# Three real products in place of four for batch 0's complex weight product, in a Fourier and maxout kernel

## The chip, the cores and the metric

The kernel runs on one core of one Trainium2 chip. The metric is the device time of one execution in microseconds (us); the time before is the median of three runs, and one further execution was profiled.

## What is computed

`x` holds 8 batches of 3072 rows by 256 columns. Each batch goes through a real Fourier transform along its rows, a complex 256 x 256 weight product with a bias, a soft threshold and the inverse transform; a maxout layer (three 256 x 768 products, their maximum, one 768 x 256 product) follows.

```
X = rfft(x, axis=1);  Xr, Xi = X.real, X.imag
Yr = Xr @ w_r - Xi @ w_i + b_r
Yi = Xr @ w_i + Xi @ w_r + b_i
Yr, Yi = sign(Y) * max(abs(Y) - 0.01, 0)      # each of the two
y = irfft(Yr + 1j * Yi, n=3072, axis=1)
h = max(y @ w1, y @ w2, y @ w3);  out = h @ w_out
```

## The kernel before

The transform of length 3072 is split as 96 x 32. For each batch the stages are: `pa`, a 96-point product along n1 (tile `a_d` in DRAM holds the result); `px`, a 32-point product along n2, in 12 groups of four frequencies; `py`, the complex weight product; the threshold; `pz`, the inverse over n2 (tile `z_d` in DRAM); `pi`, the inverse over n1; then `pu` and `pd`, the maxout layer. Batches 1 to 7 work with pairs of f16 tiles. Batch 0 goes ahead of everything in f32, because the scales that the f16 pairs need don't exist yet, and while it runs the weights are loaded (`rw`, `ru`) and put into shape by VectorE, GpSimd and ScalarE. Nothing of the maxout layer can begin before batch 0's inverse, so TensorE passes through the 12 groups of batch 0 first, and the 1630 us after them are the eight maxout layers with batches 1 to 7 woven in.

One step of batch 0's loop issues, for group k: `first_b(k+1)` (the `px` matmuls, and two ScalarE copies into `tf`, one of them negated), `first_w(k)` (eight `py` matmuls: for each of two halves j and each of two row blocks h one with `w_r` and one with `w_i`; VectorE then adds `bias` at L750, ScalarE makes the two halves of the threshold at L760 and L761, VectorE subtracts them at L762) and `first_q(k-1)` (one `pz` matmul over all 128 rows; ScalarE copies it to `zs` and sends it to `z_d`). The last group, k = 11, has its own matrices. Every engine works through its own list in order; the order within a list was fixed when the program was built, and a table (`planned(k, ...)`) says at which step the work on the maxout weights is handed in. That work has four phases for each pair of weight blocks: GpSimd scales a copy (L402, `lower`), VectorE joins the two words of a float64 (L408 and L411, `combine`; L416, `join`), and `finish` subtracts one weight from another on VectorE (L423) and splits the difference into f16 halves.

The PSUM tiles of this part are handed out in turn from three pools, `ff`, `up` and `dn`, with 3, 3 and 2 banks: a tile of `dn` takes the bank of the tile six places before it, one of the others that of the tile nine places before.

Of the kernel before, what the change touches and what calls it, by code (L numbers as in the profile page):

```python
# [25 lines left out]
def dft_tables():  # L26
# [51 lines left out]
    mq = [np.block([[u, z], [z, v]])[order] for u, v in ((q, q), (q, qs))]  # L78
    even, odd = (np.pad(fa[0:48, np.arange(96) % 4 // 2 == i], ((0, 16), (0, 16))) for i in (1, 0))
# [22 lines left out]
def fourier_maxout_kernel(  # L102
# [5 lines left out]
    P = 128  # L108
# [94 lines left out]
    qf = const.tile([P, 2, P], F32, name="qf")  # L203
# [47 lines left out]

    def load_tables():
        rows = [b.rearrange("(r o d) -> r o d", r=1, o=1) for b in (b_r, b_i)]
# [5 lines left out]
        nc.sync.dma_start(out=st["tiled"], in_=mq[:, 26])  # L259

    def load_last_bias():
        rows = [b.rearrange("(r o d) -> r o d", r=1, o=1) for b in (b_r, b_i)]
        for c in range(2):
            nc.sync.dma_start(out=bias[64 * c:64 * c + 64, 1:2], in_=rows[c].broadcast_to([64, 1, D]))
        nc.gpsimd.dma_start(out=bias[96:97, 1:2], in_=rows[0])
# [59 lines left out]
    def scale_bias():  # L325
        mb = small("mxb")
        nc.vector.tensor_reduce(
            out=mb, in_=bias[:, 0], axis=AX.X, op=ALU.max, apply_absolute_value=True
# [25 lines left out]
    class Weights:  # L354
# [33 lines left out]
        def phases(self, n):  # L388
# [30 lines left out]

            def finish():  # L420
                if self.less:
                    other = self.raw[n + 2][:, :, :, 1].bitcast(F32)
                    nc.vector.tensor_tensor(out=m, in0=m, in1=other, op=ALU.subtract)  # L423
                split_scaled(hi, lo, m, self.sc)

            return (lower, combine, join, finish) if hi is not None else (lower, combine, join)
# [285 lines left out]
    def first_b(k):  # L712
        aj = st.pop(("a", k))
        px = ff_tile("px")
        pv = px.rearrange("p (h j m) -> p h j m", h=KD, j=2)
        for j in range(2):
            for h in range(KD):
                nc.tensor.matmul(
                    pv[:, h, j], aj[:, j, h * P:(h + 1) * P], mb_f[:, 2 * k + j], start=True, stop=True
                )  # L720
        st["t", k] = t = fft.tile([P, KD, 384], F32, name="tf", tag="t2", bufs=2)
        tv = t.rearrange("p h (j m) -> p (h j) m", j=2)
# [7 lines left out]
        if k == NJP - 1:  # L730
            st["ts"] = s_tile("tsf").rearrange("p (h m) -> p h m", h=KD)
            st["late"] = nc.gpsimd.tensor_copy(out=st["ts"], in_=t[:, :, 192:320])
            for z in (32, 96):
                nc.gpsimd.memset(st["ts"][:, :, z:z + 1], 0.0)

    def first_w(k):
        last = k == NJP - 1
        t = st.pop(("t", k)).rearrange("p h (j m) -> p h j m", j=2)
        py = ff_tile("py")
        pv = py.rearrange("p (j d) -> p j d", j=2)  # L740
        for j in range(2):
            for h in range(KD):
                t2 = st["ts"][:, h] if last and j == 1 else t[:, h, j, 0:P]
                r, i = (fft_weights[h][:, n * D:n * D + D] for n in range(2))
                nc.tensor.matmul(pv[:, j], t[:, h, j, 64:192], r, start=h == 0, stop=False)
                nc.tensor.matmul(pv[:, j], t2, i, start=False, stop=h == KD - 1)
        u = fft.tile([P, 2, D], F32, name="uf", tag="vh", bufs=3)
        bv = bias if last else bias[:, 0:1, :].broadcast_to([P, 2, D])
        mx = batch(0, "u")
# [18 lines left out]
    def first_q(k):  # L768
        u = st.pop(("v", k))
        pz = ff_tile("pz")  # L770
        pv = pz.rearrange("p (j d) -> p j d", j=2)
        if k < NJP - 1:
            nc.tensor.matmul(pz, qf[:, 0], u.rearrange("p j d -> p (j d)"), start=True, stop=True)
        else:
# [757 lines left out]
```

## Time and profile before

| | us |
|---|---|
| median of three runs | 1742.47 (1741.91 to 1744.53) |
| the profiled execution, its own time | 1737.65 |
| its span, first to last instruction | 1735.9 |
| TensorE busy | 1713.4 (99%) |
| VectorE busy | 1269.0 (73%) |
| ScalarE busy | 1169.1 (67%) |
| GpSimd busy | 292.2 (17%) |

Busy shares are means over the whole span; what one stage waits for is read from the rows further down. PE is TensorE, PEld its weight loads, DVE VectorE, ACT ScalarE, POOL GpSimd, SP SyncE (DMA issues only). An f32 matmul leaves two records, one for each of its two passes.

### The profile page before, as it was taken

The page shows a single profiled execution, that of the slowest core. Times are in us where ns is not written, and L with a number is a line of the kernel's source. Part 1 is how long each engine was busy: PE and PEld are TensorE (multiplying, and loading weights), DVE is VectorE, ACT ScalarE, POOL GpSimd, SP SyncE. Part 2 cuts the span into 40 slices and gives each one's busy share as a digit, 9 for nine tenths or more (in the row PEclk, how much of TensorE's full clock was granted, in tenths as well). Part 3 has the DMA queues.
Part 4 walks back from the last instruction along what each step waited for, and adds up shares of the span by engine and source line. Part 5 has one row for each costly group of instructions (what it writes and reads, how often), then busy time and mean ns, then how long its engine had stood idle before and what let it go on. Part 6 is the DMA issues. An engine that isn't in the chain of part 4 may idle for free.

```text
span 1735.9 us, 42087 instructions
## 1 busy us (share of the span) xinstructions
PE 1713.4 (99%) x16171; PEld 1278.0 (74%) x16171; DVE 1269.0 (73%) x2690; ACT 1169.1 (67%) x2493; POOL 292.2 (17%) x523
## 2 busy tenths in 40 slices
PE   8999999999999999999999999999999999999998
PEld 5866777677776777777777777777777777778998
DVE  2887887687866788678876688757787467667775
ACT  4567676677766777667775777667776566666775
POOL 2101012111221212211221111211222110110000
PEclk9999999999999999999999999999999999999999
DMA  9866565577646767466766567555753443422121
GB/s 294 249 183 195 161 167 162 159 183 190 186 120 178 181 185 192 133 175 177 191 168 167 156 178 204 159 143 153 191 160 106 121 126 104 122 78 64 56 60 34
DMA packets 203863, 269.61 MB, mean 155 GB/s; under 512 B 31438, under 2 KB 153262, under 8 KB 203566
## 3 DMA queue, kind: packets, MB, share of 16 engines
q1 hardware_dynamic: 171294, 193.34, 42.4%
q0 software_dynamic: 24736, 66.62, 12.0%
q10 hardware_dynamic: 7632, 6.95, 1.4%
q8 instruction: 128, 2.10, 0.5%
q14 instruction: 73, 0.60, 0.1%
HBM read 124.31 MB, written 75.50 MB: 115 GB/s over the span
## 4 chain that ended last, share of the span: by engine, by line
PE 81%; DVE 9%; DMA 5%; ACT 4%; issue 1%; SPq 1%; ACTq 0%; POOL 0%; DVEq 0%; POOLq 0%
PE pu L184 11%; PE pu L186 11%; PE pu L185 11%; PE pd L184 8%; PE pd L186 8%; PE pd L185 8%; PE py L184 3%; PE py L186 3%; PE py L185 3%; PE pi L1091 2%; PE px L792 2%; PE pa L625 2%; PE pz L960 2%; PE pu L1176 2%; PE pa L642 1%
## 5 line engine op out<-in xcount | busy, mean ns | idle before, releaser
L184 PE MATMUL pu<-yh,wuh 128*128 128x384 f16 x1344 | 438.6, 326 | 0.0
L186 PE MATMUL pu<-yh,wul 128*128 128x384 f16 x1344 | 438.0, 326 | 0.0
L185 PE MATMUL pu<-yl,wuh 128*128 128x384 f16 x1344 | 438.0, 326 | 0.0
L184 PE MATMUL pd<-woh,hh 128*128 128x256 f16 x1152 | 314.1, 273 | 0.6 <-ACT o L1273 0.4
L186 PE MATMUL pd<-woh,hh 128*128 128x256 f16 x1152 | 313.8, 273 | 0.1
L185 PE MATMUL pd<-wol,hh 128*128 128x256 f16 x1152 | 313.8, 273 | 0.0
L176 DVE TENSOR_TENSOR hh<-h,hh 128x384 f16<-128x384 f32 x336 | 185.9, 553 | 110.2 <-ACT hh L175 109.9
L1142 ACT ACTIVATE pu<-pu 128x384 f32<-128x384 f32 x336 | 160.7, 478 | 145.1 <-PE pu L186 135.1
L175 ACT ACTIVATE hh<-h 128x384 f16<-128x384 f32 x336 | 174.4, 519 | 70.2 <-DVE h L1146 64.9
L186 PEld LDWEIGHTS <-wul 128*128 128x128 f16 x1344 | 131.4, 98 | 86.7
L635 POOL DMA_DIRECT2D a_d<-aq x160 | 94.9, 597 | 584.9 <-ACT aq L632 573.5
L184 PEld LDWEIGHTS <-wuh 128*128 128x128 f16 x1344 | 131.3, 98 | 83.3 <-issue 21.6
L1278 POOL DMA_DIRECT2D out_dram<-o x189 | 104.5, 559 | 449.2 <-ACT o L1273 446.0
L185 PEld LDWEIGHTS <-wuh 128*128 128x128 f16 x1344 | 131.4, 98 | 62.5 <-issue 1.0
L1150 ACT ACTIVATE h<-pu 128x384 f32<-128x384 f32 x226 | 109.4, 484 | 47.1 <-PE pu L186 42.7
L184 PE MATMUL py<-wch,tt 128*128 128x256 f16 x504 | 137.4, 273 | 0.6 <-ACT aq L632 0.3
L186 PE MATMUL py<-wch,tt 128*128 128x256 f16 x504 | 137.3, 273 | 0.0
L185 PE MATMUL py<-wcl,tt 128*128 128x256 f16 x504 | 137.3, 272 | 0.0
L184 PEld LDWEIGHTS <-hh 128*128 128x128 f16 x1152 | 112.6, 98 | 33.0 <-issue 11.8
L185 PEld LDWEIGHTS <-hh 128*128 128x128 f16 x1152 | 112.7, 98 | 21.5 <-issue 0.5
L1105 DVE SCALAR_TENSOR_TENSOR y<-pi,ye 128x192 f32<-128x192 f32 x252 | 110.4, 507 | 21.8 <-ACT ye L1099 21.6
L186 PEld LDWEIGHTS <-hh 128*128 128x128 f16 x1152 | 112.6, 98 | 13.8 <-DVE hh L176 0.4
(288 smaller groups left out, 3551.0 us busy)
## 6 DMA issues: line engine op xcount, KB each, us to landing
zq<-z_d SPq DMA_DIRECT2D x63, 384.0 KB, 4.7
out_dram<-o POOLq DMA_DIRECT2D x189, 128.0 KB, 3.5
ab<-a_d SPq DMA_DIRECT2D x84, 256.0 KB, 4.3
ab<-ab SPq DMA_DIRECT2D x336, 64.0 KB, 2.8
vb<-vb SPq DMA_DIRECT2D x308, 64.0 KB, 2.9
z_d<-zs POOLq DMA_DIRECT2D x70, 256.0 KB, 3.9
xm<-in_x_dram SPq DMA_DIRECT2D x40, 384.0 KB, 4.3
a_d<-aq POOLq DMA_DIRECT2D x160, 96.0 KB, 3.3
```

Of the source, the lines that this page charges most:

```text
L175: nc.scalar.activation(out=hi, in_=src, func=AF.Copy)
L176: later(lambda: nc.vector.tensor_tensor(out=lo, in0=src, in1=h, op=ALU.subtract))
L184: nc.tensor.matmul(o, lh, rh, start=start, stop=False, **kw)
L185: nc.tensor.matmul(o, lh, rl, start=False, stop=False, **kw)
L186: st["mm"] = nc.tensor.matmul(o, ll, rh, start=False, stop=stop, **kw)
L625: st["mm"] = nc.tensor.matmul(pa[r][64 * h:64 * h + 64], ft[rows, t], xt[rows, i, h], start=t == i, stop=t == 1,)
L635: nc.gpsimd.dma_start(out=av[1 - r, :, :, n:n + 512], in_=o[64 * h:64 * h + 48])
L792: nc.tensor.matmul(pv[:, h, :, g // 2, g % 2], ah[:, g // 2, g % 2, h * P:(h + 1) * P], mb_sb[:, i, 4 * kb + g].rearrange("p (c m) -> p c ...
L1105: nc.vector.scalar_tensor_tensor(out=yv[:, e], in0=pv[:, 0], scalar=(1 - 2 * e) * Y_SCALE, in1=ev, op0=ALU.mult, op1=ALU.add,)
L1142: st["act"] = nc.scalar.activation(out=p, in_=p, func=AF.Relu)
L1150: st["act"] = nc.scalar.activation(out=h32, in_=p, func=AF.Relu, scale=H_SCALE)
L1278: nc.gpsimd.dma_start(out=out_v[b, c, t + i], in_=o[:, i])
```

## The change

For groups 0 to 10 of batch 0 the complex product is made from three real ones: (Xr + Xi) times `w_r`, Xi times -(`w_r` + `w_i`), and Xr times (`w_i` - `w_r`). `add_fft_weights` makes the two sums of weights on VectorE. GpSimd makes Xr + Xi (L745). The first product (`pc`) is copied out by ScalarE (`cs`, L772), GpSimd adds it to the bias (L774), and VectorE adds the two others (L800). The real and imaginary parts now lie side by side in the columns, so the inverse over n2 is four matmuls on 64 rows each, two into each of two PSUM tiles, and it runs two groups behind instead of one. The subtraction of maxout weights goes from VectorE to GpSimd (L436), and the table of planned work has new numbers. Group 11 keeps its form.

```
 def first_b(k):
...
+    if k < NJP - 1:
+        pv = px.rearrange("p (h c j m) -> p h j c m", h=KD, c=2, j=2)
...
+    if k < NJP - 1:
+        nc.scalar.activation(out=t[:, :, 0:256], in_=px.rearrange("p (h m) -> p h m", h=KD), func=AF.Copy)
+        nc.gpsimd.tensor_tensor(
+            out=t[:, :, 256:384], in0=t[:, :, 0:128], in1=t[:, :, 128:256], op=ALU.add
+        )
+        return
...
+def first_sum(k):
+    pc = ff_tile("pc")[:, 0:D]
+    first_product(pc, st["t", k], 2, [fft_weights[h][:, 0:D] for h in range(KD)])
+    c1 = s_tile("cs")
+    nc.scalar.activation(out=c1, in_=pc, func=AF.Copy)
+    st["u", k] = u = fft.tile([P, 2, D], F32, name="uf", tag="vh", bufs=3)
+    nc.gpsimd.tensor_tensor(
+        out=u, in0=bias_ri, in1=c1.rearrange("p (o d) -> p o d", o=1).broadcast_to([P, 2, D]), op=ALU.add
+    )
...
+        first_sum(k)
+        t, bv = st.pop(("t", k)), st.pop(("u", k))
+        pv = py.rearrange("p (c d) -> p c d", c=2)
+        first_product(pv[:, 0], t, 1, st["ws"][0])
+        first_product(pv[:, 1], t, 0, st["ws"][1])
...
 def first_q(k):
     u = st.pop(("v", k))
-    pz = ff_tile("pz")
-    pv = pz.rearrange("p (j d) -> p j d", j=2)
     if k < NJP - 1:
-        nc.tensor.matmul(pz, qf[:, 0], u.rearrange("p j d -> p (j d)"), start=True, stop=True)
...
+        pz = [ff_tile("pz")[:, 0:D] for _ in range(2)]
+        for c in range(2):
+            for j in range(2):
+                rows = slice(64 * j, 64 * j + 64)
+                nc.tensor.matmul(pz[j], qf[rows, 2 + c], u[rows, c], start=c == 0, stop=c == 1)
+        return pz
...
-        for c in range(2):
-            nc.sync.dma_start(out=bias[64 * c:64 * c + 64, 0:1], in_=rows[c].broadcast_to([64, 1, D]))
-        nc.sync.dma_start(out=qf, in_=mq[:, 0:2])
+        for c, v in enumerate((b_r, b_i)):
+            row = v.rearrange("(o d) -> o d", o=1)
+            nc.sync.dma_start(out=bias_ri[:, c], in_=row.broadcast_to([P, D]))
+        nc.sync.dma_start(out=qf, in_=mq[:, 0:4])
...
-    for n in range(0, 6, 2):
-        planned(n - 1, phase, w_up, n)
-        planned(n, prepare, w_up, n)
-        if n < 4:
-            planned(5 + n // 2, phase, w_up, n)
+    for k, n in ((1, 0), (2, 2), (5, 4)):
+        planned(k - 1, phase, w_up, n)
+        planned(k, prepare, w_up, n)
+    for k, n in ((4, 0), (6, 2)):
+        planned(k, phase, w_up, n)
+    for k, n in ((6, 0), (7, 2)):
+        planned(k, phase, w_up, n)
...
-        (load_a, k + 3), (load_a, k + 4), (stage_b, k + 1), (stage_w, k), (finish_w, k), (stage_q, k - 1),
+        (load_a, k + 3), (load_a, k + 4), (stage_b, k + 1), (stage_w, k), (finish_w, k), (stage_q, k - 2),
+        (stage_q, k - 1 if k == NJP else -1),
```

VectorE's list at the beginning of batch 0's loop, before: L750 adds the bias to `py` of a group, L373 finds the largest value of a loaded weight block `rw`, L762 ends the threshold (rows that only read an accumulator are left out here and below).

```order
L750 ISA uf_278,mxu_279<-py_269,bias_89 128x512
L373 TENSOR_REDUCE mwu_96<-rw_241 128x2
L762 ISA uf_278,mxu_279<-uf_278,t_281 128x512
L750 ISA uf_321,mxu_279<-py_312,bias_89 128x512
L373 TENSOR_REDUCE mwu_96<-rw_254 128x2
```

The same place after the change, from the first weight block to the end of group 0's threshold; L800 is now the addition of the bias, L812 the end of the threshold, and the names of `rw` are those of the first three blocks and then the fourth.

```order
L387 TENSOR_REDUCE mwu_96<-rw_245 128x2
L387 TENSOR_REDUCE mwu_96<-rw_258 128x2
L387 TENSOR_REDUCE mwu_96<-rw_300 128x2
L422 TENSOR_SCALAR xhl_303<-xhl_303 128x768
L422 TENSOR_SCALAR xhl_354<-xhl_354 128x768
L425 SCALAR_TENSOR_TENSOR rw_245<-rw_245,xhl_303 128x768
L425 SCALAR_TENSOR_TENSOR rw_258<-rw_258,xhl_354 128x768
L800 ISA uf_278,mxu_271<-py_272,uf_278 128x512
L430 SCALAR_TENSOR_TENSOR rw_245<-rw_245 128x768
L800 ISA uf_321,mxu_271<-py_315,uf_321 128x512
L387 TENSOR_REDUCE mwu_96<-rw_348 128x2
L812 ISA uf_278,mxu_271<-uf_278,t_285 128x512
```

Before, group 0's addition stood ahead of the first weight block; now three blocks' maxima and four passes over the first two stand ahead of it.

TensorE's list around group 0's inverse, before: `py_312` is group 1's product (its last two of eight matmuls), `pz_327` group 0's inverse, `pt_334` a small transpose for a scale, `px_357` group 3 and `py_365` group 2.

```order
L745 MATMUL py_312<-wst_132,tf_266 128x256
L746 MATMUL py_312<-wst_132,tf_266 128x256
L773 MATMUL pz_327<-uf_278,qf_73 128x512
L278 MATMUL pt_334<-id_sb_76,col_288 128x128
L718 MATMUL px_357<-mb_all_77,aj_244 128x128 x4
L745 MATMUL py_365<-wst_132,tf_309 128x256
```

The same place after the change: `py` and `pc` of groups 0, 1 and 2 are 272 and 273, 315 and 316, 366 and 367, `px` of groups 3 and 4 is 358 and 403, and pz_383 and pz_384 are group 0's inverse.

```order
L764 MATMUL py_315<-wch_79,tf_268 128x256 x4
L292 MATMUL pt_332<-id_sb_76,col_292 128x128
L764 MATMUL pc_273<-wst_132,tf_255 128x256 x2
L764 MATMUL pc_316<-wst_132,tf_268 128x256 x2
L764 MATMUL py_366<-wch_79,tf_312 128x256
L764 MATMUL pc_367<-wst_132,tf_312 128x256
L738 MATMUL px_358<-mb_all_77,aj_248 128x2x64 x4
L764 MATMUL pc_367<-wst_132,tf_312 128x256
L764 MATMUL py_366<-wch_79,tf_312 128x256 x3
L738 MATMUL px_403<-mb_all_77,aj_261 128x2x64
L825 MATMUL pz_383<-uf_278,qf_73 128x256
L825 MATMUL pz_384<-uf_278,qf_73 128x256
```

Group 0's inverse stood right behind group 1's `py`; it has moved behind `pc`, `px` of group 3 and the whole of group 2's product.

GpSimd's list after the change, from its first addition on: L745 makes a group's sum in `tf` (255, 268 and 312 are groups 0 to 2), L416 is the scaling of a weight block that was L402, L774 adds the bias.

```order
L745 TENSOR_TENSOR tf_255<-tf_255 128x2x128
L745 TENSOR_TENSOR tf_268<-tf_268 128x2x128
L416 TENSOR_SCALAR xhl_303<-rw_245 128x768
L416 TENSOR_SCALAR xhl_354<-rw_258 128x768
L774 TENSOR_TENSOR uf_278<-bias_ri_90,cs_276 128x512
L416 TENSOR_SCALAR xhl_500<-rw_300 128x768
L745 TENSOR_TENSOR tf_312<-tf_312 128x2x128
L774 TENSOR_TENSOR uf_321<-bias_ri_90,cs_319 128x512
```

Before, the list held only the L416 rows (as L402) here; group 2's sum now stands behind the scaling of the third weight block.

## Rows read from the trace of the kernel before

**Rows 1.** Busy us (instructions) by stretch: PE, PEld, DVE, ACT, POOL, clock, DMA, GB/s.
```profile
30.00:40.00 10.00, 10.00 (x56) 8.69 (x55) 4.31 (x12) 4.85 (x12) 0.91 (x1) 1.00 1.04 369
50.00:60.00 10.00, 10.00 (x49) 8.01 (x49) 10.00 (x20) 5.54 (x10) 2.27 (x3) 1.00 1.01 347
```

**Rows 2.** TensorE's waits from 29 to 104 us: total, times, longest, in us.
```profile
PE pz L773 <- DVE mxu L762: 1.0, 1, 1.0
PE pi L1041 <- ACT zh L1028: 0.5, 1, 0.5
```

**Rows 3.** TensorE's timeline: start, us, instruction; batch 0's loop and its end.
```profile
29.14 2.02 PE L718 MATMUL px<-mb_all,aj 128*128 128x128 f32 x16 [3.25 <-DMA aj<-a_d]
31.00 0.66 PE L745 MATMUL py<-wst,tf 128*128 128x256 f32 x2
...
78.43 1.05 PE L718 MATMUL px<-mb_all,aj 128*128 128x128 f32 x8
79.32 0.60 PE L745 MATMUL py<-wst,tf 128*128 128x256 f32 x2
...
82.78 1.02 PE L773 MATMUL pz<-uf,qf 128*128 128x512 f32 x2
83.63 0.38 PE L278 MATMUL pt<-id_sb,col 128*128 128x128 f32 x2
...
103.81 0.91 PE L1041 MATMUL pi<-xm,zh 96*128 96x96 f16 x11 [0.53 <-ACT zh L1028]
```

**Rows 4.** TensorE's timeline around matmuls on 48 of 128 rows, four places of the array.
```profile
336.89 0.27 PE L186 MATMUL pd<-woh,hh 128*128 128x256 f16 x1
337.09 0.84 PE L625 MATMUL pa<-xhl,zeros 48*64 48x512 f16 x12
337.86 0.34 PE L184 MATMUL pu<-yh,wuh 128*128 128x384 f16 x1
```

**Rows 5.** DMA issues from 33.2 to 33.6 us: size, us to landing.
```profile
rw<-in_moe_w_dram SPq DMA_DIRECT2D x1, 768.0 KB, 9.5
```

**Rows 6.** VectorE's timeline from 42 to 50 us, and one row later on.
```profile
42.83 0.94 DVE L373 TENSOR_REDUCE mwu<-rw 128x2 f32<-128x768 f32 x1
43.69 1.02 DVE L408 TENSOR_SCALAR xhl<-xhl 128x768 uint32<-128x768 uint32 x2
44.62 0.95 DVE L411 SCALAR_TENSOR_TENSOR rw<-rw,xhl 128x768 uint32<-128x768 uint32 x1
45.49 0.68 DVE L750 CUSTOM_DVE_ANT_1 uf<-py,bias 128x512 f32<-128x512 f32 x1
...
49.03 0.68 DVE L762 CUSTOM_DVE_ANT_0 uf<-uf,t 128x512 f32<-128x512 f32 x1
49.64 0.95 DVE L416 SCALAR_TENSOR_TENSOR rw<-rw 128x768 uint32<-128x768 uint32 x1
...
64.02 1.39 DVE L762 CUSTOM_DVE_ANT_0 uf<-uf,t 128x512 f32<-128x512 f32 x1
```

**Rows 7.** GpSimd's timeline: two of its instructions.
```profile
36.41 0.91 POOL L402 TENSOR_SCALAR xhl<-rw 128x768 f32<-128x768 f32 x1 [11.31 <-DMA rw<-in_moe_w_dram]
...
63.73 1.14 POOL L402 TENSOR_SCALAR xhl<-rw 128x768 f32<-128x768 f32 x1 [1.88 <-DVE ru L411]
```

**Rows 8.** ScalarE's groups, 20 to 104 us: busy us, mean ns, idle before.
```profile
L945 ACT ACTIVATE zs<-pz 128x512 f32<-128x512 f32 x12 | 7.1, 590 | 13.5 <-PE pz L773 13.0 <-issue 0.4
L726 ACT ACTIVATE tf<-px 128x256 f32<-128x256 f32 x12 | 4.5, 377 | 0.0
```

**Rows 9.** TensorE's timeline in its first 26 us, and stretches at the span's end.
```profile
1.32 4.02 PE L1297 MATMUL idle<-zeros 128*128 128x512 f16 x9 [1.32 <-POOL zeros L1292]
20.11 5.78 PE L1297 MATMUL idle<-zeros 128*128 128x512 f16 x26
...
1731.00:1733.00 2.00, 0.21 (x2) 0.00 (x0) 0.48 (x1) 0.84 (x2) 0.00 (x0) 1.00 0.02 6
1733.00:1735.90 2.90, 0.00 (x0) 0.00 (x0) 0.00 (x0) 0.00 (x0) 0.00 (x0) 0.75 0.39 132
```

More of the change, by code (lines that the diff above doesn't have):

```diff
@@ L263, in load_last_bias @@
         for c in range(2):
-            nc.sync.dma_start(out=bias[64 * c:64 * c + 64, 1:2], in_=rows[c].broadcast_to([64, 1, D]))
+            for j in range(2):
+                nc.sync.dma_start(
+                    out=bias[64 * c:64 * c + 64, j:j + 1], in_=rows[c].broadcast_to([64, 1, D])
+                )
         nc.gpsimd.dma_start(out=bias[96:97, 1:2], in_=rows[0])
@@ L327, in scale_bias @@
         nc.vector.tensor_reduce(
-            out=mb, in_=bias[:, 0], axis=AX.X, op=ALU.max, apply_absolute_value=True
+            out=mb, in_=bias_ri.rearrange("p c d -> p (c d)"), axis=AX.X, op=ALU.max, apply_absolute_value=True
         )
@@ L729, in first_b @@
         )
[L730 to L734, printed above, removed]
+        st["ts"] = s_tile("tsf").rearrange("p (h m) -> p h m", h=KD)
+        nc.gpsimd.tensor_copy(out=st["ts"], in_=t[:, :, 192:320])
+        for z in (32, 96):
+            nc.gpsimd.memset(st["ts"][:, :, z:z + 1], 0.0)
@@ new lines, in first_product @@
+    def first_product(o, t, part, w):
+        for h in range(KD):
+            nc.tensor.matmul(
+                o, t[:, h, part * P:(part + 1) * P], w[h], start=h == 0, stop=h == KD - 1
+            )
+    def first_sum(k):
[6 more added lines that the diff above has]
+            out=u, in0=bias_ri, in1=c1.rearrange("p (o d) -> p o d", o=1).broadcast_to([P, 2, D]), op=ALU.add
+        )
@@ L736, in first_w @@
     def first_w(k):
         last = k == NJP - 1
-        t = st.pop(("t", k)).rearrange("p h (j m) -> p h j m", j=2)
+        mx = batch(0, "u")
         py = ff_tile("py")
[L740 to L746, printed above, removed]
@@ L747, in first_w @@
-        u = fft.tile([P, 2, D], F32, name="uf", tag="vh", bufs=3)
-        bv = bias if last else bias[:, 0:1, :].broadcast_to([P, 2, D])
-        mx = batch(0, "u")
+        if last:
+            t = st.pop(("t", k)).rearrange("p h (j m) -> p h j m", j=2)
+            pv = py.rearrange("p (j d) -> p j d", j=2)
+            for j in range(2):
+                for h in range(KD):
+                    t2 = st["ts"][:, h] if j == 1 else t[:, h, j, 0:P]
+                    r, i = (fft_weights[h][:, n * D:n * D + D] for n in range(2))
+                    nc.tensor.matmul(pv[:, j], t[:, h, j, 64:192], r, start=h == 0, stop=False)
+                    nc.tensor.matmul(pv[:, j], t2, i, start=False, stop=h == KD - 1)
+            u = fft.tile([P, 2, D], F32, name="uf", tag="vh", bufs=3)
+            bv = bias
+        else:
+            first_sum(k)
[3 more added lines that the diff above has]
+            first_product(pv[:, 1], t, 0, st["ws"][1])
+            u = bv
@@ L1384, in fourier_maxout_kernel @@
                 pump()
-    with tc.issue_after(st["late"].ins):
-        for c, v in enumerate((b_r, b_i)):
-            row = v.rearrange("(o d) -> o d", o=1)
-            nc.gpsimd.dma_start(out=bias_ri[:, c], in_=row.broadcast_to([P, D]))
     quiet = st["power"].ins, st["zs"].ins
```

59 lines of the change are left out of this document (38 added, 21 removed).

## The prediction

> **What bounds the kernel now.** I read the busy time by stretch first [rows 1]. While batch 0's groups run, TensorE is busy in all of each 10 us at clock 1.00; VectorE fills its stretch as well from 50 to 60 us, and the DMA engines are at a share of 1.0 at 347 to 369 GB/s. The waits [rows 2] say who decides: between 29 and 104 us TensorE waits 1.0 us once for VectorE's L762 and 0.5 us once for the first `pi`, besides the wait for its first data. So batch 0's part lasts as long as TensorE's own matmuls, from 29.14 us to the first `pi` at 103.81 [rows 3]. Behind that TensorE is busy 99% of the span, so a shift of the first `pi` should reach the end nearly whole. In a group [rows 3] four `px` take 0.89 us (78.43 to 79.32), eight `py` 3.46 (79.32 to 82.78), thus 0.433 for one of 256 columns, and `pz` with 512 columns 0.85 (82.78 to 83.63). The reader is to see that this is a TensorE bound with VectorE close behind, so a saving on TensorE counts only while no other engine is late.
>
> **1. Six products for eight.** Two fewer in each of 11 groups: 22 x 0.433 = **-9.5 us**.
>
> **2. The inverse.** One matmul of 512 columns (0.85) becomes four of 256 columns on 64 rows. Each has two passes of 0.216 (half of 0.433). No row of before shows f32 on 64 rows. The nearest [rows 4] are twelve f16 matmuls of 512 columns, each at one of four places of the array: they take 0.77 us (337.09 to 337.86), where one after the other would take 12 x 0.22 = 2.7 (26 such on the full array take 5.78 [rows 9]); so matmuls at different places do overlap, three rounds of 0.22 being 0.67, and 0.1 is lost, with another 0.1 ahead (336.89 to 337.09 for a spacing of 0.11). Bounds for the four: 0.86, if the two halves of the array work side by side throughout (no cost), and 1.73 + 0.2 = 1.93, if they don't at all: 11 x 1.08 = +11.9. I take the middle way. TensorE starts matmuls in order, and both passes of one use the same rows, so the next one, on the other rows, can start only with the second pass; four then need five pass times, 1.08, plus 0.2 for the change to and fro: 1.28, 11 x 0.43 = **+4.7 us**. On this the Trainium skill (TensorE: Matmul & The Clock Gate, Part 3) says that matmuls on distinct row groups run concurrently, some 4 ns apart. No run here shows that for f32; by it the four would cost 0.86 + 0.2, the term would be +2.3, and the sum 2.4 us lower.
>
> **3. The start of the loop.** Here I put most of the time, because the list of VectorE has changed. Its first L800 (group 0's bias, once L750 behind group 0's `py`) now stands behind the maximum of the third weight block, two L422 and two L425. The third block was issued at 33.2 to 33.6 and took 9.5 us to land [rows 5]; VectorE read it at 42.83 [rows 6]. Ahead of it SyncE now asks for 256 KB more (both biases on 128 rows instead of 64, 128 KB, and twice the `qf`, 128 KB): at 369 GB/s [rows 1] 0.7 us, so 43.5. Then, by the starts in [rows 6], 0.86 for the maximum, 0.93 for two L422 (as L408), 2 x 0.87 for two L425 (as L411), 0.61 for L800: group 0's addition ends at **47.6**. Before, the addition of group 2 already began at 45.49.
>
> TensorE gets there earlier. From 31.00 [rows 3]: `py` of group 0 1.73, `px` 0.89, `py` of group 1 1.73, `pt` 0.2, four `pc` 1.73, and one `py` of group 2, whose `tf` ScalarE writes behind `pc` of group 0: about 38.0. The next `pc` needs group 2's sum, which GpSimd makes behind the scaling of the third block (43.5 + 0.9 [rows 7] + some 0.6). Then `px` of group 3 needs a PSUM bank: counted through the program (`px` and `py` of group 0 are the 19th and 21st tile, and so on), it is the 27th, in `dn`, and takes the bank of the 21st, `py` of group 0, which L800 sets free at 47.6. So TensorE stands from 38.0 to 47.6 but for one `pc`: **+9.2 us** (8.5 if the extra bytes delay nothing, 10.2 if GpSimd slows VectorE by 1 us here). Behind it `pz` of group 0 needs L812: 47.6 + 0.87 (L430, as L411) + 0.61 + 0.86 + 0.68 = 50.6, about when TensorE comes to it.
>
> **4. The old waits go.** With TensorE late, L762's 1.0 us goes; all ten `pa` matmuls (0.85 each) now stand behind the last `pz`, where eight left 0.5 us uncovered: **-1.5 us** (to 0).
>
> **5. Waits later on.** Followed further by the same durations, both lists stay close: `pc` of group 4 takes the bank of `py` of group 3, and comes 0.9 us before its L800. The other banks and the `pz` have 2 to 5 us in hand. **+1.0 us** (0 to 4, rival C).
>
> **6. The clock.** The trace's one low clock is at its end [rows 9]: after the last matmul, 0.2 us into 1731 to 1733, the stretch 1733.00 to 1735.90 has 0.75, a mean of 1.00 and the lower of the two levels, 1.2 GHz. The idle time at 26 us, 3.25 us long [rows 3], kept 1.00. The new one has 7 us without a matmul, so I expect the clock at 1.2 GHz when work resumes. What that costs is seen at the program's start [rows 9]: nine matmuls of 512 columns in 4.02 us, 0.45 each instead of 0.22. Some 4 us at half speed lose **+2.0 us** (0, if it stays up, to 2.8, if all of the 2.8 us ahead of group 0's `pz` takes twice as long).
>
> **What costs nothing.** The four weight sums on VectorE fall ahead of the loop; even from 30 to 40 us it is busy only 4.31 us [rows 1]. ScalarE [rows 8] loses one copy of 256 columns, gains one (0.38), and copies `pz` in two (2 x 0.38 for 0.59): 0.2 us more a group beside TensorE's 4.8; it is busy half of its time [rows 1]. If that cover went, it would be 2 us. GpSimd's two additions of 256 and 512 columns a group are two-input operations that no row shows: below as its one-input rows (0.91 for 768 columns [rows 7], so 0.9 for both), above twice that; I take 1.8, by its doubled input. They have the 3.9 us in which TensorE works at other groups; where GpSimd's list stands, as in step 3, that cover is gone, and `pc` waits. The subtraction by GpSimd spares VectorE two operations of 0.9 us (as L411) in the loop, where after step 3 it is no longer what TensorE waits for. Of the DMAs, the four for the last bias and the moved `z_d` stores come where nobody waits.
>
> **The sum**: -9.5 + 4.7 + 9.2 - 1.5 + 1.0 + 2.0 = **+5.9 us**. Against the profiled execution's own 1737.65 that is 1743.5; the median of the runs lies 4.8 above that execution, and there the forecast is **1748.4**.
>
> **Rivals.**
> A, *no slower after all*: the two halves of the array work side by side. Then step 2 is +0 to 2.3 and, if the clock also holds and no wait follows, the sum is -9.5 + 0 + 9.2 - 1.5 = -1.8: about 1740.7. For it speaks that f16 did overlap [rows 4]; against it the order in which TensorE starts passes. It decides below about 0.95 us for the four.
> B, *one after the other*: step 2 is +11.9, the sum +13.1, 1755.6. For it: no f32 row on half of the array; against it [rows 4].
> C, *VectorE becomes the bound from 50 to 75 us*: while GpSimd ran from 63.73 to 64.87, an L762 took 1.39 instead of 0.68 [rows 6, 7], and GpSimd now works some 10 us between 50 and 64. If half of that time is added to VectorE (+5), TensorE, with 2 to 3 us in hand, waits 3 more: sum +9, 1751.5. The Trainium skill (GPSIMD Engine Reference, Key points) names this: GpSimd shares its SBUF interfaces with VectorE, and they contend where VectorE has two SBUF inputs. By that rule, the trace agrees.
> D, *faster*: the wait of step 3 doesn't come, since the weights land by 36 us. Then -9.5 + 4.7 = -4.8, 1737.7. Against it: the landing of 42.7 [rows 5, 6], with DMA at a share of 1.0.
>
> **How the numbers follow.** A measurement of this kernel can tell 0.2% (3.5 us) from no change. Chances: the forecast 0.50, of which 0.07 end within 3.5 us; A 0.15, all within; B 0.15; C 0.13; D 0.07, faster. So faster 0.07, same 0.22, slower 0.71. The range leaves out D and the upper part of B: **1740.5 to 1756**; the forecast's own is 1745 to 1752.
>
> **What would show it.** Step 1: six matmuls of `py` and `pc` a group, 2.6 us. Step 2: from the start of `pz` to the next `px` 1.28 us (0.9 to 1.1 for A, 1.9 for B). Step 3: a gap on TensorE from 38 to 47 us, put down to GpSimd and to L800, and the first L800 ending near 47.6, after the third maximum. Step 6: a clock below 1.00 in 40 to 50 us. Step 5 and C: waits of `pc` or `pz` for VectorE between 50 and 75, L812 far above 0.69. The first `pi` should come at about 109.5. Wrong it would be if the gap is under 5 us, or if VectorE's first L800 ends before 43.

## The result, and the profile after

The changed kernel takes 1761.62 us (median of 5 runs, 1760.29 to 1765.71) where the one before takes 1742.38 (5 runs, 1741.48 to 1744.53): a ratio of 1.0116, 95% interval 1.0105 to 1.0127, some 20 us slower. The profiled executions are 1760.29 and 1737.65 us. Differences in us below are (ratio - 1) times 1742, each kernel against the runs of before beside it.

The first `pi` begins at 124.55 us, 20.7 later than before [rows 3]; so the loss is nearly all in batch 0's loop, and what follows hands it on to the end. The waits of TensorE in the loop, after, answer to [rows 2]:

```profile
PE pc L764 <- POOL tf L745: 17.0, 5, 12.3
PE px L738 <- DMA aj<-a_d: 3.3, 1, 3.3
PE pc L764 <- DVE mxu L800: 2.9, 1, 2.9
PE pz L829 <- DVE mxu L892: 0.8, 1, 0.8
```

TensorE waits 17 us for a sum that GpSimd alone makes in 0.73 (0.89 in the mean here). VectorE, for its part, waits 11.6 us for GpSimd's addition of the bias (the group's row from 30 to 124 us, with busy us, mean ns and idle before):

```profile
L800 DVE CUSTOM_DVE_ANT_0 uf<-py,uf 128x512 f32<-128x512 f32 x11 | 7.6, 687 | 11.6 <-POOL uf L774 11.6
```

TensorE's timeline, after (start, us), answers to [rows 3]:

```profile
37.89 0.70 PE L764 MATMUL py<-wch,tf 128*128 128x256 f32 x2
50.84 1.22 PE L764 MATMUL pc<-wst,tf 128*128 128x256 f32 x2 [12.25 <-POOL tf L745]
...
57.99 1.03 PE L764 MATMUL pc<-wst,tf 128*128 128x256 f32 x4
58.85 1.89 PE L764 MATMUL py<-wch,tf 128*128 128x256 f32 x8
60.67 1.14 PE L825 MATMUL pz<-uf,qf 64*128 64x256 f32 x8
61.74 1.16 PE L738 MATMUL px<-mb_all,aj 128*128 128x128 f32 x8
62.73 1.03 PE L764 MATMUL pc<-wst,tf 128*128 128x256 f32 x4
...
71.46 1.84 PE L764 MATMUL pc<-wst,tf 128*128 128x256 f32 x4 [3.60 <-POOL tf L745]
...
97.68 1.13 PE L764 MATMUL pc<-wst,tf 128*128 128x256 f32 x4 [2.85 <-DVE mxu L800]
...
124.55 0.92 PE L1096 MATMUL pi<-xm,zh 96*128 96x96 f16 x11
```

Where nothing waits (57.99 to 62.73) a group takes 4.74 us, before 5.20. What the gap of 12.25 us waits for is read from GpSimd's timeline and from VectorE's:

```profile
43.27 1.26 POOL L774 TENSOR_TENSOR uf<-bias_ri,cs 128x512 f32<-128x512 f32 x1
47.87 1.52 POOL L416 TENSOR_SCALAR xhl<-rw 128x768 f32<-128x768 f32 x1 [3.33 <-DVE rw L425]
49.35 1.43 POOL L745 TENSOR_TENSOR tf<-tf 128x256 f32<-128x256 f32 x1
```

```profile
45.02 0.95 DVE L387 TENSOR_REDUCE mwu<-rw 128x2 f32<-128x768 f32 x1 [1.68 <-DMA rw<-in_moe_w_dram]
45.89 1.02 DVE L422 TENSOR_SCALAR xhl<-xhl 128x768 uint32<-128x768 uint32 x2
46.82 1.82 DVE L425 SCALAR_TENSOR_TENSOR rw<-rw,xhl 128x768 uint32<-128x768 uint32 x2
48.56 0.68 DVE L800 CUSTOM_DVE_ANT_0 uf<-py,uf 128x512 f32<-128x512 f32 x1
...
62.87 2.02 DVE L430 SCALAR_TENSOR_TENSOR rw<-rw 128x768 uint32<-128x768 uint32 x1
```

Group 2's sum (49.35) stands behind the scaling of the third weight block, and that waits for VectorE's L425: `xhl` has two buffers, and the first comes free only when the first L425 has read it, at about 47.7. L425 waits for its turn behind the maximum of the third block, read at 45.02. So one late block held VectorE, through it GpSimd, and through that TensorE. While GpSimd works beside them, operations of VectorE with two operands in SBUF stretch: that L430 takes 2.02 us, alone 0.95. How they do is read further down, where the lists are equal.

Busy time and clock by stretch, after (columns as in [rows 1]):

```profile
40.00:50.00 10.00, 0.00 (x0) 0.00 (x0) 6.51 (x10) 0.71 (x1) 4.79 (x5) 0.55 1.05 392
50.00:60.00 10.00, 9.16 (x44) 7.93 (x45) 6.29 (x14) 4.08 (x9) 7.00 (x6) 0.77 0.81 262
70.00:80.00 10.00, 8.28 (x36) 6.45 (x37) 10.00 (x20) 2.86 (x6) 8.22 (x7) 0.83 0.62 174
90.00:100.00 10.00, 7.14 (x37) 5.62 (x37) 3.61 (x10) 4.99 (x11) 3.21 (x3) 0.95 0.44 128
100.00:110.00 10.00, 10.00 (x52) 7.56 (x51) 4.37 (x18) 5.71 (x13) 3.77 (x6) 0.88 0.38 87
```

The clock is below 1.00 behind each of the three long waits, and VectorE, full from 50 to 60 us before [rows 1], is now busy 6.29 us there while it is waited for: the bound is a chain across engines and no longer one engine.

### The profile page after: what moved, and what is told of

Read it like the earlier page. It is cut to its first block, busy times and chain, and to the rows that moved or that the text cites. A ratio compares the mean times of both kernels' runs of the same rounds, so it can differ in the third digit from the quotient of the medians.

```text
span 1758.5 us, 42204 instructions
## 1 busy us (share of the span) xinstructions
PE 1715.0 (98%) x16193; PEld 1276.3 (73%) x16193; DVE 1274.0 (72%) x2690; ACT 1169.9 (67%) x2504; POOL 324.6 (18%) x547
## 4 chain that ended last, share of the span: by engine, by line
PE 80%; DVE 8%; ACT 4%; DMA 4%; issue 2%; SPq 1%; POOL 1%; ACTq 0%; DVEq 0%; POOLq 0%
PE pu L185 11%; PE pu L187 11%; PE pu L186 11%; PE pd L185 8%; PE pd L187 8%; PE pd L186 8%; PE py L185 3%; PE py L187 3%; PE py L186 3%; PE pi L1146 3%; PE px L845 2%; PE pa L642 2%; PE pu L1231 2%; PE pz L1015 2%; PE pa L659 1%
```

## The experiments

**The order of the weight work.** Three kernels put the work on the maxout weights behind the loop's own. The core of the edit (`sum` is L745, `add` is L800; the first kernel also plans the maxima and the phases later, the second has `sum` alone, the third `add` alone):

```
+            with ExitStack() as behind:
+                for e in ("sum", "add"):
+                    if k >= 0:
+                        behind.enter_context(tc.issue_after(st[e].ins))
+                for fn, args in plan[k]:
+                    fn(*args)
...
-        planned(-2 + n // 2, w_up.largest, n)
+        planned(n // 2, w_up.largest, n)
```

Both lists, and later: 

> The changed kernel with one thing moved: the work on the maxout weights stands behind the loop's own work. VectorE takes the maxima of the weight blocks two steps later and works on a step's blocks only behind that step's L800, and GpSimd scales and subtracts only behind L745 of the next group. Nothing is left out. Theory (order): the loss of the change is that TensorE waited for L745 behind L416 behind L425 behind a weight block, 12.25 us at 38 to 51 us, then 3.6 and 2.85 us, with the clock falling after each. Then the gap from 38 to 51 us should go (under 2 us of it left), the clock stay at 1.00 from 40 to 110 us, the first pi come at about 98 (124.55 less 20.7 of waits less some 5.7 of low clock), and the time be some 1736, below both kernels. Rival (the new operations are too slow where they run: contention of GpSimd and VectorE, 64-row matmuls): waits of like size come back at other places between 50 and 110 us, and the time stays above 1750. In between, the six products are worth less than 22 x 0.433 us.

Measured: 1.0099 (1.0082 to 1.0116), +17 us. The gap of 12.25 us is gone (1.65 is left), and still only some 3 us are gained, no more than the two intervals leave open: with that rest, five waits for L745 make 12.4 us, and two of `pt` 4.0, at other places. TensorE's timeline at the largest, then ScalarE's just before it:

```profile
48.68 1.16 PE L738 MATMUL px<-mb_all,aj 128*128 128x128 f32 x8
53.41 1.65 PE L764 MATMUL pc<-wst,tf 128*128 128x256 f32 x4 [3.57 <-POOL tf L745]
```

```profile
50.60 0.59 ACTq L1004 DMA_DIRECT2D z_d<-zs  x1
51.24 0.72 ACT L811 ACTIVATE uf<-uf,mlam 128x512 f32<-128x512 f32 x1 [3.48 <-DMA rw<-in_moe_w_dram]
51.87 0.58 ACT L744 ACTIVATE tf<-px 128x512 f32<-128x512 f32 x1
```

Here the sum is late because ScalarE's copy to `tf` stands behind a `z_d` store. ScalarE's list stood still for 3.48 us around the issue of that store (0.59 us); the profile puts the wait down to the landing of a weight block, and no run shows why a store should wait for it. My first theory, that the start of the loop is the loss, falls.

GpSimd's list alone: 

> The changed kernel with GpSimd's list alone moved: the weight work that a step hands in stands behind L745 of the next group; VectorE's list is left to the program. Theory (order): group 2's sum no longer waits for the third scaling, but L800 of group 0 still stands behind three maxima and some of the work on the first block on VectorE, so px of group 3 waits for its bank until about 47.9 in place of pc until 50.8: 3 us less, and more if the waits at 71 and 97 us go as well (up to 9): 1752 to 1759. Rival (contention): the waits depend on how long the operations take and not on their order, so no more than 1 us is gained.

Measured: 1.0091 (1.0076 to 1.0107), +16 us, in the upper part of the range that the theory (order) gave: some 4 us less than the changed kernel, where the intervals leave 1 to 8 open. The gap came in two parts (3.8 and 4.7 us), and a wait of 6.0 us for L745 came at 82 us. What stands ahead of that one shows the rival at work, on VectorE (L140 splits a weight, 1.02 us each before, as L139) and on GpSimd, at the same time:

```profile
77.15 2.86 DVE L140 SCALAR_TENSOR_TENSOR wul<-rw,swu,wuh 128x768 f16<-128x768 f32 x1
```

```profile
76.60 2.60 POOL L436 TENSOR_TENSOR rw<-rw 128x768 f32<-128x768 f32 x1
79.16 2.00 POOL L774 TENSOR_TENSOR uf<-bias_ri,cs 128x512 f32<-128x512 f32 x1
```

VectorE's list alone: 

> The changed kernel with VectorE's list alone moved: the weight work that a step hands in stands behind that step's L800; GpSimd's list is left to the program. Theory (order): L800 of group 0 ends at about 44, and group 2's sum stands behind the second scaling only (42.4 + 0.9), one L774 (1.3) and itself (0.7): TensorE resumes at about 45.4 in place of 50.8. 5 us less, and more if later waits go: 1752 to 1757. Rival (the chain on GpSimd is what counts, VectorE's order does not): no more than 1 us is gained. If both this kernel and the one with GpSimd's list moved gain, either engine alone was enough to hold TensorE.

Measured: 1.0103 (1.0085 to 1.0122), +18 us, with waits of 9.1 us for L745 and 6.2 for L800; the 2 us of gain are less than the intervals can tell. Neither list alone, nor both, gives back more than some 4 of the 20 us.

**The inverse alone**, on the kernel before:

```
-            nc.tensor.matmul(pz, qf[:, 0], u.rearrange("p j d -> p (j d)"), start=True, stop=True)
...
+            pz = [ff_tile("pz")[:, 0:D] for _ in range(2)]
+            for c in range(2):
+                for j in range(2):
+                    rows = slice(64 * j, 64 * j + 64)
+                    nc.tensor.matmul(pz[j], qf[rows, 0], u[rows, c], start=c == 0, stop=c == 1)
...
```

> The kernel before with the inverse alone changed: pz of groups 0 to 10 is four matmuls of 256 columns on 64 rows into two PSUM tiles, and two copies by ScalarE. The four take their rows so that two accumulate in each tile as in the changed kernel; the sum over the other 64 rows is left out, so the output is another one. By the trace after (a group's pz takes 1.07 us in place of 0.85): +2.3 us, 1744.7. By the prediction's step 2 (1.28 us): +4.7, 1747.1. One after the other: +11.9, 1754. If the extra tile in the rotation of banks makes a wait, up to 1 us more.

Measured: 1.0035 (1.0024 to 1.0047), +6.1 us. TensorE's timeline in it:

```profile
43.92 0.59 PE L746 MATMUL py<-wst,tf 128*128 128x256 f32 x2
44.44 1.13 PE L775 MATMUL pz<-uf,qf 64*128 64x256 f32 x8
45.51 1.16 PE L718 MATMUL px<-mb_all,aj 128*128 128x128 f32 x8
46.50 0.60 PE L745 MATMUL py<-wst,tf 128*128 128x256 f32 x2
...
50.05 1.14 PE L775 MATMUL pz<-uf,qf 64*128 64x256 f32 x8
```

The four take 1.07 us, two by two side by side: their records start in pairs, 7 ns apart (44.442 and 44.449, 44.762 and 44.769, and so on), here as in the trace after. But there is 0.09 ahead of them (43.92 + 0.43 to 44.44) and `px` takes 0.99 in place of 0.89. A group lasts 5.61 us (44.44 to 50.05), 0.41 more than before: 11 x 0.41 = 4.5. The other 1.6 us are within the interval; in this trace TensorE waits 1.6 us for L762 where there was 1.0, and 1.7 for a later `pi`.

**GpSimd's additions, waited for by nobody, and left out.** The first kernel lets L774 write to a spare buffer:

```
-        first_product(pc, st["t", k], 2, [fft_weights[h][:, 0:D] for h in range(KD)])
+        first_product(pc, st["t", k], 0, [fft_weights[h][:, 0:D] for h in range(KD)])
...
-            out=u, in0=bias_ri, in1=c1.rearrange("p (o d) -> p o d", o=1).broadcast_to([P, 2, D]), op=ALU.add
+            out=other[:, k % 2], in0=bias_ri, in1=c1.rearrange("p (o d) -> p o d", o=1).broadcast_to([P, 2, D]), op=ALU.add
...
-            t, bv = st.pop(("t", k)), st.pop(("u", k))
+            t, u, bv = st.pop(("t", k)), st.pop(("u", k)), bias_ri
```

> The changed kernel with all of GpSimd's additions kept, but with nobody waiting for them: the first product takes Xr in place of Xr + Xi, and L800 adds the bias alone, while L774 writes into a spare buffer. So the third product's share is left out of the result; matmuls, copies and GpSimd's work are the same in number and size. Theory (chain: TensorE loses its time waiting for GpSimd's sum, and VectorE for GpSimd's addition, because both stand in order among the weight work): -9.5 + 4.6 us against the kernel before with next to no waits, 1736 to 1741. Rival (contention: GpSimd's additions slow VectorE, whoever waits for them): VectorE is late from 50 to 75 us, and the time stays at 1748 or above.

> As the kernel in which nobody waits for GpSimd's additions, and the 22 additions left out altogether (L745 and L774; the result lacks the third product's share). Both theories: no chain and no contention but that of the four subtractions by GpSimd, so 1736 to 1741. The difference to the kernel that keeps the additions without waiting for them is the contention alone: under 2 us by the chain theory, 8 us or more by the rival.

Measured: with the additions 1.0063 (1.0046 to 1.0080), +11.0 us; without them 0.9989 (0.9976 to 1.0002), -1.9. So 22 additions that nobody waits for cost 12.9 us. (ScalarE still waits for GpSimd once, 1.7 us.) From there to the changed kernel's 20.2 it is 9.2 more; the waits for the additions are in it, but these two kernels' lists differ too, so that the 9.2 are not the waits alone. VectorE's groups from 30 to 115 us, first with the additions, then without (us in sum, mean ns; L805 is L812 there):

```profile
L812 DVE CUSTOM_DVE_ANT_0 uf<-uf,t 128x512 f32<-128x512 f32 x11 | 10.7, 975 | 8.2 <-ACT uf L811 8.2
L425 DVE SCALAR_TENSOR_TENSOR rw<-rw,xhl 128x768 uint32<-128x768 uint32 x6 | 8.3, 1377 | 0.0
```

```profile
L805 DVE CUSTOM_DVE_ANT_0 uf<-uf,t 128x512 f32<-128x512 f32 x11 | 8.4, 765 | 5.5 <-ACT uf L804 5.4
L425 DVE SCALAR_TENSOR_TENSOR rw<-rw,xhl 128x768 uint32<-128x768 uint32 x6 | 5.7, 950 | 0.0
```

**In one order.** The lists of the two had come out differently (weight work ahead of L800 of group 2 only where the additions are). So each was run once more with VectorE's, ScalarE's, TensorE's and SyncE's instructions put in the other's order:

```
+    for e, order in ORDER.items():
+        traced = [i for i in nc.cur_bb.bb.instructions if str(i.engine) == "EngineType." + e]
+        for a, b in zip(order, order[1:]):
+            tc.add_manual_dep(
+                traced[b], traced[a].name,
+                mybir.DependencyInfo(mybir.DependencyClass.NoSync, mybir.DependencyReason.DATA), reason="order",
+            )
```

> The kernel without GpSimd's 22 additions (1740.3), but with its instructions on VectorE, ScalarE, TensorE and in the DMA queue of SyncE put one for one into the order of the kernel that keeps them without waiting for them (1753.1); the order had differed, since it is found anew for each program. The share of the third product is left out, as there. Contention: the additions themselves cost, so 1738 to 1742. Order: the worse place of the weight work in VectorE's list costs, so 1750 to 1754. A part of each: in between, and the part is read off.

> The counterpart: GpSimd's 22 additions kept without anybody waiting for them, and the order on VectorE, ScalarE, TensorE and in SyncE's queue that of the kernel without them. Contention: 1751 to 1755. Order: 1738 to 1742. If the two kernels of one order differ as much in both orders, the difference is contention alone.

| us against before | without the additions | with them | their cost |
|---|---|---|---|
| order of the kernel without | -1.9 | +5.4 | 7.3 |
| order of the kernel with | +5.1 | +11.0 | 5.9 |
| cost of the order | 7.0 | 5.6 | |

(Ratios 1.0029, 1.0018 to 1.0040, and 1.0031, 1.0018 to 1.0045, for the two new ones; by the intervals each of the four costs is known to some 3 us.) So about half of the 12.9 us is the additions themselves, at equal lists of the other engines, and about half is the order that a program with them was given.

At equal lists VectorE's instructions can be compared one by one. From 30 to 112 us, the same 111 of them take 63.9 us with the additions and 58.9 without in the order of the kernel with, and the same 113 take 65.8 and 59.5 in the other: VectorE's own stretch, 5.1 and 6.3 us, is about what the additions cost. L812, L425 and L430, with two operands in SBUF, make 2.5 and 6.4 us of it, L422 makes 2.4 and -0.2; L800, which reads PSUM, and L387 stay the same within 0.04 us. Here is L812 in the two new kernels, with the additions in the order of the kernel without (L815), and without them in the order of the kernel with (L808):

```profile
L815 DVE CUSTOM_DVE_ANT_0 uf<-uf,t 128x512 f32<-128x512 f32 x11 | 12.6, 1141 | 6.9 <-ACT uf L814 6.7
```

```profile
L808 DVE CUSTOM_DVE_ANT_0 uf<-uf,t 128x512 f32<-128x512 f32 x11 | 10.1, 919 | 8.1 <-ACT uf L807 8.1
```

So at equal lists its mean goes from 765 to 1141 ns, and from 919 to 975. The 919 ns without any addition say that a part of the order's cost is the same stretch, beside GpSimd's work on the weights.

How the stretch comes about is read from the longest case, with the additions in the order of the kernel without: VectorE's L815, then GpSimd's subtraction (L439), sum (L748) and addition of the bias (L778).

```profile
56.75 3.87 DVE L815 CUSTOM_DVE_ANT_0 uf<-uf,t 128x512 f32<-128x512 f32 x1 [1.78 <-ACT uf L814]
```

```profile
55.99 2.19 POOL L439 TENSOR_TENSOR rw<-rw 128x768 f32<-128x768 f32 x1
58.12 0.73 POOL L748 TENSOR_TENSOR tf<-tf 128x256 f32<-128x256 f32 x1
58.80 1.26 POOL L778 TENSOR_TENSOR wcl<-bias_ri,cs 128x512 f32<-128x512 f32 x1
```

L815 (0.69 us alone) began while L439 ran, stood until the third of three operations in a row had ended at 60.06, and ended 0.56 us behind it; `pz` then waited 2.5 us for it. In this trace, in that of the additions in their own order and in that of the changed kernel, all 14 L812 that took more than 0.77 us end 0.54 to 0.56 us behind a GpSimd operation. The reverse is there too: the changed kernel's L774 of 62.36, begun beside an L812 that ended at 62.94, ended 1.13 us behind that, at 64.07. So in these traces the later of two such operations ends as if its work began only when the earlier had ended, and GpSimd's next one can go ahead of a VectorE operation that still stands.

**Contention on the kernel before.**

```
...
+        nc.gpsimd.tensor_tensor(out=other[:, 0, 0], in0=u[:, 0], in1=u[:, 1], op=ALU.add)
+        nc.gpsimd.tensor_tensor(out=other[:, 1], in0=u, in1=u, op=ALU.add)
```

> The kernel before with two additions by GpSimd in each of groups 0 to 10 that nobody needs, of the sizes of the change (256 and 512 columns), made from the finished threshold of the group and written to a spare buffer. The result is that of before. Theory (chain): within 0.2% of before. Rival (contention): VectorE is full from 40 to 70 us, and some 10 us of GpSimd's additions fall there; if half to all of that is added to VectorE, TensorE, 2 to 3 us ahead of it, waits 2 to 8 us: 1744 to 1750.

Measured: 1.0035 (1.0019 to 1.0050), +6.1 us, in the rival's range. But the lists were not held here, and VectorE's came out in another order (L411 of the first weight block now stands behind L750, for one), so order can have a part in it. L762 did not stretch (770 ns in the mean, 792 before); L408 went from 548 to 833 ns, L411 from 950 to 1105. VectorE also waited 2.9 us for the additions themselves, at 89 and 98 us, but TensorE did not wait for it there. TensorE now waits 5.1 us for L762 where it waited 1.0:

```profile
PE pz L776 <- DVE mxu L762: 5.1, 3, 2.6
```

**All of it by VectorE**, and then one kind at a time (`nc.gpsimd` becomes `nc.vector` in L745, L774 and L436).

> The changed kernel with its new work for GpSimd given to VectorE: the sum L745, the addition L774 and the subtraction of weights. GpSimd then works as in the kernel before, and nothing is left out. Contention alone: no overlap of new work, so VectorE pays 11 x (0.43 + 0.68) + 2 x 0.9 = 14 us of its own, of which what fits into its idle time from 70 us on is free: 1742 to 1750. Chain: the same chain now runs through VectorE's list, where weight work stands too, and TensorE waits for VectorE as it did for GpSimd: 1752 to 1760.

Measured: 1.0020 (1.0009 to 1.0032), +3.5 us, in the range of contention: without the new work of GpSimd, 17 of the 20 us are gone. VectorE takes 0.48 us for the sum, 0.74 for the addition and 0.95 for a subtraction; GpSimd alone 0.73, 1.26 and 2.15. The waits of `pc` for the sum fall from 17.0 to 4.0 us:

```profile
PE pc L764 <- DVE tf L745: 4.0, 3, 1.5
PE px L738 <- DMA aj<-a_d: 3.4, 2, 3.2
PE pc L764 <- ACT zs L1000: 1.4, 1, 1.4
```

The sum alone: 

> The changed kernel with the sum Xr + Xi alone (L745) made by VectorE. All three kinds of work back on VectorE gave -17.9 us (1743.8). If TensorE's waits for the sum (17.0 us in the trace after) are the loss: nearly all of it, 1745 to 1749. If the loss goes by GpSimd's busy time (sum 8 us, bias 14, subtractions 9 us of 31): a quarter, 1756 to 1758.

The addition of the bias alone: 

> The changed kernel with the addition of the bias alone (L774) made by VectorE. By GpSimd's busy time: 14 of 31 us, so -8, 1752 to 1755. If the sum is what counts: within 2 us of 1761.6.

The subtraction alone: 

> The changed kernel with the subtraction of weights alone (L436) back on VectorE, as before the change. By GpSimd's busy time: 9 of 31 us, so -5, 1755 to 1758. If the sum is what counts: within 2 us of 1761.6, or above it, since VectorE has two operations of 0.95 us more in the loop.

Measured: the sum 1.0046 (1.0031 to 1.0062), 12 us less than the changed kernel; the addition 1.0074 (1.0053 to 1.0094), 7 less; the subtraction 1.0100 (1.0082 to 1.0118), 3 less. Together they would be 22, and all at once gave 17. The sum counts most, above its share of GpSimd's time and below "nearly all"; the addition counts by its share. The 3 us of the subtraction are within the intervals, and the lists were found anew in each of the three, so a part of each gain can be order.

**The clock.** 104 matmuls without use in the gap:

```
+        if k == 3:
+            for _ in range(104):
+                nc.tensor.matmul(st["pc"], zeros[:, 0:P], zeros[:, 0:D], start=True, stop=True)
```

> The changed kernel with 104 matmuls of 256 columns in f16 that nobody needs, in TensorE's idle time from 38 to 50 us, and all lists else in the changed kernel's order; the result is the same. They keep TensorE busy up to 1 us before the sum comes. Step 6 (the clock): the granted clock stays at 1.00 from 50 to 60 us, where it was 0.77, 4.6 us at half speed, so 2.3 us less: about 1759.3. If the later engines decide anyway, TensorE only waits longer at its next waits, and the time stays within 1 us of 1761.6.

What ran was not what this describes: the lists were found anew, and the 104 stood behind the wait for the sum, where they held TensorE for 13.71 us. It took 1.0174 (1.0159 to 1.0190), some 10 us more than the changed kernel, and says nothing on the clock. Again, with the lists held:

> The changed kernel with 104 matmuls of 256 columns in f16 that nobody needs, put between the first matmul of group 2's py and its pc, where TensorE stands idle from 38 to 50 us, and with all five lists else in the changed kernel's order, one for one; the result is the same. Each took some 0.11 us at the full clock, so they end at about 50, before the sum comes at 50.8. Step 6: the granted clock is 1.00 from 50 to 60 us, where it was 0.77, 4.6 us at half speed: 2.3 us less, about 1759.3, and TensorE reaches the next waits earlier. If the later engines decide anyway: within 1 us of 1761.6.

Measured: 1.0113 (1.0094 to 1.0132), +19.7 us against 20.2: no change. The stretch with the clock at 1.00, and the timeline:

```profile
50.00:60.00 10.00, 10.00 (x72) 8.75 (x70) 6.95 (x14) 4.43 (x8) 8.45 (x6) 1.00 1.02 321
```

```profile
41.55 11.52 PE L736 MATMUL pc<-zeros 128*128 128x256 f16 x104
52.90 0.60 PE L770 MATMUL pc<-wst,tf 128*128 128x256 f32 x2
...
72.92 2.07 PE L770 MATMUL pc<-wst,tf 128*128 128x256 f32 x4 [3.69 <-POOL tf L751]
```

The 2.3 us of the expectation are within the interval, so the trace decides. TensorE now runs at full speed from 52.90 on, but from the end of the gap to the end of the next long wait for GpSimd it takes 20.0 us (52.90 to 72.92) where it took 20.6 (50.84 to 71.46): of what the clock gives back, 0.6 us is left behind the next wait. The two later falls were not tried.

**A version for use.** On top of all three kinds by VectorE, `pc` last and read from PSUM; then the same with the weight work later.

```
-        c1 = s_tile("cs")
-        nc.scalar.activation(out=c1, in_=pc, func=AF.Copy)
...
-        nc.gpsimd.tensor_tensor(
-            out=u, in0=bias_ri, in1=c1.rearrange("p (o d) -> p o d", o=1).broadcast_to([P, 2, D]), op=ALU.add
+        nc.vector.tensor_tensor(
+            out=u, in0=bias_ri, in1=pc.rearrange("p (o d) -> p o d", o=1).broadcast_to([P, 2, D]), op=ALU.add
```

> A version for use, with the result in full: three products, the sum, the addition of the bias and the subtractions of weights all by VectorE; the first product comes last of the three, and VectorE adds the bias to it straight from PSUM, which saves ScalarE's copy. Against the kernel with all of it on VectorE (1743.8), TensorE's 4.0 us of waits for the sum and 1.4 us for ScalarE should go, and VectorE, nearly full from 50 to 80 us, gains nothing: 1739 to 1743. Below 1738.5 (0.2% under before) only if VectorE's list has room to spare; the kernel that leaves these additions out altogether stands at 1740.3, which speaks against it.

> The version with all additions by VectorE and the first product last (1740.65), with the weight work moved to later steps behind each step's L800 and sum; result in full. If order is what it still loses, its 7 us of waits shrink by half: 1736 to 1738, faster than before by over 0.2%. If VectorE's time is: 1740 or above.

Measured: 0.9992 (0.9983 to 1.0002) and 0.9991 (0.9980 to 1.0001): level with before. Moving the weight work gained nothing here, so its place is not what this version still loses. No version that I ran is faster by more than the measurement tells.

## Why the prediction was wrong

It had the sign, and 5.9 us where 20.2 were measured. By its steps:

- **The bound**: right. TensorE sets the pace, and its saving counts only while no other engine is late. That condition is what broke.
- **Step 1**, -9.5: right. `pc` and `py` of a group take 2.6 us in place of 3.46. The kernel without additions (-1.9) and the inverse alone (+6.1) leave some -8 for it, within 3 us.
- **Step 2**, +4.7: the sum is right (4.5), by luck, since two errors cancel. The matmuls on the two halves of the array go side by side, four passes of 0.216 or 0.86 us where I had five, 1.08. The change to and fro costs 0.4 us and not 0.2: 0.21 within the 1.07, 0.09 ahead of them and 0.10 in the `px` behind. On the overlap the Trainium skill (TensorE: Matmul & The Clock Gate, Part 3), by which matmuls on distinct row groups run concurrently, some 4 ns apart, was right where I took the middle way; the records here are 7 ns apart.
- **Step 3**, +9.2: the right place, too small, by a missed wait. "The next `pc` needs group 2's sum, which GpSimd makes behind the scaling of the third block (43.5 + 0.9 [rows 7] + some 0.6)": the sum ended at 50.78, not 45. The scaling also needed a buffer that VectorE's L425 gave back at about 47.7, and the block itself was read at 45.02, since SyncE issued it at 35.32 and not at 33.25. First L800: predicted end 47.6, measured 49.2. But the experiments on the order show that this gap, taken alone, is worth little: without it, others come.
- **Step 4**, -1.5: right. The waits for L762 and for the first `pi` went; a wait of 0.8 us in the last group (L829 for L892) is new.
- **Step 5**, +1.0, rival C and **what costs nothing**: here the prediction failed. It followed both lists with the durations of before and gave GpSimd's additions 3.9 us of cover a group. The duration of the additions was about right (0.73 + 1.26 for 1.8 taken). That they run beside VectorE was priced only in rival C, at 3 us of waits, and is worth 5.9 to 7.3 at equal lists; beside VectorE they take 0.89 and 1.40 themselves in the mean. That they stand in the chain was given 1.0: TensorE waits for GpSimd's sum five times and VectorE 11.6 us for its addition. TensorE's waits behind the first gap are 8.5 us (17.0 + 2.9 + 0.8 - 12.25). "The subtraction by GpSimd spares VectorE two operations" is true of the count, but L815 above stood 1.4 us beside such a subtraction, and giving it back did not cost what it had spared (3 us less, within the intervals).
- **Step 6**, +2.0: the clock fell three times, not once; by the stretches (0.77, 0.83, 0.95, 0.88) 11.4 us ran at half speed, 5.7 us of TensorE's time. The price was right: two matmuls of `pc` took 1.64 us (71.46 to 73.10) for 0.86 (57.99 to 58.85). (The rows at the program's start, from which it was taken, are at a clock that the profile gives as 1.00, so they did not show it by themselves.) Up to the first `pi` the terms then add up: -9.5 + 4.5 + 20.7 of waits - 1.5 + 5.7 = 19.9, for 20.7 measured. But a term of such a sum is not a cause: with the first fall taken away, most of what it had cost went into the next wait.

What caused the 20.2 us, by what was run: the products and the inverse, with the rest of the plan, -1.9; GpSimd's additions beside VectorE, 6 to 7; the order that the lists got with them, 6 to 7, each to some 3 us; the other 9 by difference, with TensorE's and VectorE's waits for the additions in them and yet another order of the lists. What stays open: how the 9 us split between these two, how the order's part splits between VectorE's and ScalarE's lists, and the later two falls of the clock.

On rival C's mechanism the runs say more. At equal lists VectorE's operations with two operands in SBUF stretched, those that read PSUM or reduce one input did not (L800 682 and 682 ns, L387 946 and 945); L422, with one input, went from 665 to 915 ns in one order and from 816 to 595 in the other. The rows that rival C cites show the same: the L762 of 64.02 ended at 65.41, 0.54 us behind GpSimd's operation that ended at 64.87. Half of GpSimd's time was no measure of that; what counts is which operations meet, and whether GpSimd's come in a row. The Trainium skill (GPSIMD Engine Reference, Key points) says that the two engines share SBUF interfaces and contend where VectorE has two SBUF inputs or runs in a 2-port performance mode. By that rule, the trace agrees on the operations with two inputs; whether L422 runs in such a mode no run shows.

## What to carry to other kernels

Work handed to an idle engine is not free if its operations hold up those of the engine close to the bound: price it at its own time and at the stretch of the other, here 6 to 7 us for 22 additions of some 2 us a pair. For the stretch, look where operations with two operands meet the other engine's: the later one ends as if it had waited for the earlier. An engine put into the chain of every group brings its whole list with it, with the buffers that its other work waits for, so follow each of those waits before giving it cover. When a gap in the trace is taken away and the time stays, the gap was slack of something else: test the cause by leaving the work out, not by moving it, and hold the lists of the other engines while you do, since a program with less work is given other lists (6 to 7 us here).

## What I had not expected of the hardware

- Four f32 matmuls of 256 columns on 64 rows each take 1.07 us in all where two on 128 rows take 0.87, with 0.1 us more ahead of them and behind.
- With GpSimd at work beside them, single operations of VectorE took 2.02 us for 0.95, 2.86 for 1.02 and 3.87 for 0.69, and GpSimd's own 2.60 for 2.15 and 2.00 for 1.26: both engines lose, and the later operation ends a fixed time behind the earlier (0.54 to 0.56 us for L812).
- ScalarE's list stood still for 3.48 us around a store that it issues, by the profile until a weight block, loaded by SyncE, had landed.
- In the changed kernel's profile the clock fell behind waits of 12.25, 3.60 and 2.85 us in the loop, while 3.29 us of idle time ahead of the loop left it at 1.00 (30 to 40 us); in that of the kernel with matmuls in the gap it was 0.83 there, behind 3.26 us. With the additions in the order of the kernel without, it fell behind 2.06 us (0.83 from 80 to 90 us); with two additions on the kernel before, 2.56 us left it at 1.00 (70 to 90 us).
